# One residual quantiser on one core: 26 rounding copies change engine, and every queue gets a new order

## The chip, the core and the metric

The kernel runs on one core of one Trainium2 chip. The metric is device time in microseconds from the start to the end of one execution; a kernel's time is the median of several executions. All data are bf16 except the sums in PSUM, which are f32.

The engines are called by the names of the profile: PE is TensorE (matrix products), PEld its weight loads, DVE is VectorE, ACT is ScalarE, POOL is GpSimd, SP is SyncE, which here only issues DMAs. Each engine takes its instructions in the order in which the program lists them, so an instruction that has to wait holds back all that stands behind it on that engine.

## The reference

`x` is 2 x 16000 x 512. A depthwise convolution of three taps and a SiLU make `z`; four codebooks of eight words each quantise it in turn, each the residual that the one before left; a second depthwise convolution of three taps decodes the sum of the chosen words.

```
z = silu(conv3(x, dw_enc))
res = z ; q = 0
for s in range(4):
    cb = codebooks[s]                         # 8 x 512
    d2 = sum(res*res) - 2*res@cb.T + sum(cb*cb)
    sel = cb[d2.argmin(-1)]
    q += sel ; res -= sel
y = conv3(q, dw_dec)
```

The squared norm of the residual takes part in the distance, rounded to bf16 as in the reference, and so can decide between words; that is why the kernel computes it.

## The kernel before, in words

The 32,000 rows are laid out as 250 groups of 128. They are worked on in 18 chunks: one of 4 groups, one of 12, thirteen of 16 (numbers 2 to 14), two of 12 (15 and 16) and one of 2 (`SIZES`). Several chunks are under way at once, in different steps:

1. **Load** (L671, SP): transposing DMAs bring a chunk in as XT, with the 512 features on partitions in four blocks.
2. **Front** (L738 to L765), for each of the four blocks: DVE makes the three products of the encoder's taps (L738). One sum of two products is made by an accumulating DMA that POOL issues (L744), the other by DVE (L746). ACT takes the exponential (L750), DVE (or ACT, L755) adds one (L757), ACT takes the reciprocal (L368), DVE multiplies (L765) into RES, the residual. Exponential and reciprocal are in different function tables, and ACT loads a table at each change.
3. **Four stages**, s = 0 to 3, on RES. PE makes products of the residual with the code words and with itself in groups of rows, into PSUM (L839, L844). What follows has two forms. In chunks of 16 groups (`apart`): ACT moves the products of the residual with itself into GRAM (L855) and the dot products into PR (L879), PE adds up both in PSUM, with L865 and L871 as its last step; so one PSUM tile holds, for each row and each of the eight words, the norm plus the dot product. **A rounding copy then takes this 128x128 tile out of PSUM into V as bf16.** In all other chunks DVE takes the norm by a reduction (L875) and adds it to PR in L922. From V on, DVE adds the words' norms (L927), takes the minimum of eight (L932) and marks where it stands (L937). PE turns the marks (L963 or L949), ACT copies them out (L972), PE makes pairs of them (L999), ACT copies these out (L1004), PE multiplies them with the code words (L1032), and DVE takes the chosen words from RES (L1039, or L1043 in small chunks), four instructions a stage. Then the next stage's products can begin. The last stage has no subtraction: its marks go on to the decoder (L976 to L989).
4. **Decode** (L1061, L1067, L1071): PE multiplies the marks with code words times decoder taps, ACT copies the result to YSB, SP stores it.

The rounding copy is the one instruction whose engine the change touches. `copied` (in `stage`) decides it: `COPIES` has one number for chunks with an even number and one for odd ones, and bit s of it says whether ACT makes the copy in stage s.

```
copied = apart and COPIES[st["n"] % 2] >> s & 1
...
if apart:
    if copied:
        nc.scalar.activation(u["V"]..., u["N"], ACT.Copy)       # L917
    else:
        nc.vector.tensor_copy(u["V"]..., u["N"])                # L919
    return
```

`apart` needs a chunk of four times four groups (`MB >= LEAST`, with `LEAST` = 4), a bit of `NORMS` (15, so all stages) and a chunk number from `NFROM` = 0 to below `NTO` = 15. With `COPIES = (5, 5)`, bits 0 and 2, ACT makes the copies of stages 0 and 2 and DVE those of stages 1 and 3: 26 each, for 13 chunks.

The order in which the program lists its steps is written out in full: each step (a product, an exponential, a stage's products of one group of rows, one subtraction, one transposing DMA) is a task with a number, and `ORDER` is a list of all 3,217 numbers. `Plan.run` goes down the list and emits each task's instructions, so the list fixes the order on every engine, SP's and POOL's DMA issues included. It also contains entries of -1, at which PE gets a matrix product without use (L612), meant to keep it busy, if one can be placed. The list must name a task after those that it needs.

```
for n in ORDER:
    if n < 0:
        self.idle()
        continue
    tasks[n][5]()
```

Buffers in turns limit how far chunks can run ahead: 2 tiles of XT, 6 of Z, 4 of T, 4 of E, 3 of RES, 2 of YSB; in PSUM 2 small tiles hold a stage's products and sums (`psG`), 3 large ones everything else (`psA`). The rounding copy is what frees the small tile in which the sums stand.

Of the kernel before, what the change touches and what calls it, by code (L numbers as in the profile page):

```python
# [63 lines left out]
NTO = 15  # L64
LEAST = 4
COPIES = (5, 5)
# [260 lines left out]
def kernel(  # L327
# [489 lines left out]
    def stage(st, s, due):  # L817
# [5 lines left out]
        seen, maxima, grams = [], [], []  # L823
        apart = MB >= LEAST and NORMS[st["n"] % 2] >> s & 1 and NFROM <= st["n"] < NTO

# [339 lines left out]
```

## Time and profile before

| | us |
|---|---|
| three executions | 654.52, 656.47, 660.09 |
| their median | 656.47 |
| the profiled execution, whole | 654.74 |
| its span, first to last instruction | 653.0 |
| in the span DVE was busy | 614.3 |
| ACT | 581.7 |
| PE | 509.0 |

The profiled execution is thus 1.73 us below the median; 1.74 us of it lie outside the span. The mean clock granted to TensorE was 0.934 of full speed.

Busy time of an engine is the time in which at least one of its instructions ran. Instructions of one engine overlap a little at their ends, so the sum of their durations is larger than the busy time; what one more instruction takes of a full queue is read from the distance between two starts. In a row of a group, the number behind the bar is the busy time of the group in us, then the mean duration of one in ns; behind the second bar stands how long the engine was idle just before such instructions, and what ended that idle time.

### The profile page before, as it was taken

Reading aid. Unit: us, or ns where it says so; the run is one execution under the profiler, and the core shown is the slowest. Engines: PE = TensorE matmul, PEld = TensorE weight load, DVE = VectorE, ACT = ScalarE, POOL = GpSimd, SP = SyncE. Lnnn points to the kernel's source line nnn. Section 1 sums busy time; section 2 is a strip of 40 time slices with the busy share of each in tenths; the row PEclk is TensorE's granted clock in tenths of the full one; section 3 lists DMA queues with packets and bytes.
Section 4 is the critical chain, followed back from the end, with each engine's and each line's share of the span. In section 5 each row is a group of like instructions: output and inputs, shape, how many; then the busy total and the mean of one; then the engine's idle time right before and its main releaser. Section 6 shows DMA issues by size and latency. Waiting matters only on the chain.

```text
span 653.0 us, 25437 instructions
## 1 busy us (share of the span) xinstructions
PE 509.0 (78%) x11302; PEld 319.6 (49%) x11389; DVE 614.3 (94%) x991; ACT 581.7 (89%) x862; POOL 93.1 (14%) x133
## 2 busy tenths in 40 slices
PE   4115674777878799888988798888779888999985
PEld 3114452534545455555655455545445555556552
DVE  7999999999989999999999999999999999999872
ACT  3887857799889999999999999999999999997576
POOL 7403111111101201011011101111111111200000
PEclk9656677989989999999999999999999999999999
DMA  9949886899898999998799989999889936242234
GB/s 202 134 93 183 150 137 128 135 156 151 167 152 148 185 207 166 192 190 182 142 230 159 158 206 164 175 182 212 148 178 166 174 92 171 86 140 72 92 140 186
DMA packets 148489, 103.33 MB, mean 158 GB/s; under 512 B 130169, under 2 KB 131194, under 8 KB 148250
## 3 DMA queue, kind: packets, MB, share of 16 engines
q1 hardware_dynamic: 137076, 65.96, 50.8%
q0 software_dynamic: 11296, 35.73, 33.1%
q8 instruction: 89, 1.46, 0.9%
q14 instruction: 22, 0.18, 0.1%
q10 hardware_dynamic: 6, 0.00, 0.0%
HBM read 3.61 MB, written 32.77 MB: 56 GB/s over the span
## 4 chain that ended last, share of the span: by engine, by line
DVE 37%; ACT 32%; PE 13%; DMA 7%; SPq 6%; issue 5%; DVEq 0%; ACTq 0%; POOLq 0%
DVE RES L1039 9%; ACT YSB L1067 8%; ACT E L368 7%; DVE T L738 6%; SPq L671 5%; ACT E L750 5%; PE PS L844 5%; PE SEL L1032 4%; DVE RES L1043 4%; DVE Z L746 4%; DVE RES L765 4%; ACT GRAM L855 3%; DMA Z<-T 3%; DMA out_dram<-YSB 3%; DVE Z L738 3%
## 5 line engine op out<-in xcount | busy, mean ns | idle before, releaser
L844 PE MATMUL PS<-RES 128*64 128x80 bf16 (+1 forms) x8064 | 187.2, 205 | 25.2 <-DVE RES L765 13.7
L844 PEld LDWEIGHTS <-RES 128*64 128x64 bf16 x8064 | 161.5, 116 | 80.9 <-issue 46.0
L1039 DVE TENSOR_TENSOR RES<-RES,SEL 128x2048 bf16<-128x2048 bf16 x156 | 186.4, 1216 | 7.8 <-PE SEL L1032 7.5
L1032 PE MATMUL SEL<-OHP,W 64*128 64x512 bf16 (+2 forms) x1296 | 157.3, 365 | 28.3 <-ACT OHP L1004 10.6
L744 POOL DMA_DIRECT2D Z<-T x72 | 69.3, 975 | 480.3 <-DVE T L738 88.1
L1067 ACT ACTIVATE YSB<-Y 128x1024 bf16<-128x1024 f32 (+1 forms) x126 | 130.2, 1049 | 7.8 <-PE Y L1061 4.8
L750 ACT ACTIVATE E<-Z 128x2048 bf16<-128x2048 bf16 (+2 forms) x72 | 122.9, 1718 | 4.2 <-DVE Z L746 3.4
L368 ACT ACTIVATE E<-E 128x2048 bf16<-128x2048 bf16 (+2 forms) x72 | 122.9, 1723 | 1.5 <-DVE E L757 1.3
L738 DVE TENSOR_SCALAR T<-XT,WENC 128x2048 bf16<-128x2048 bf16 (+2 forms) x144 | 97.3, 686 | 2.1 <-DMA Z<-T 2.1
L1032 PEld LDWEIGHTS <-W 64*128 64x128 bf16 x1296 | 57.2, 97 | 80.1 <-issue 43.9
L765 DVE TENSOR_TENSOR RES<-Z,E 128x2048 bf16<-128x2048 bf16 (+2 forms) x72 | 78.2, 1086 | 0.1
L855 ACT ACTIVATE GRAM<-PS 128x384 bf16<-128x384 f32 (+1 forms) x156 | 73.0, 489 | 5.6 <-PE PS L844 5.4
L746 DVE TENSOR_TENSOR Z<-Z,T 128x2048 bf16<-128x2048 bf16 (+2 forms) x72 | 74.3, 1040 | 1.0 <-DMA Z<-T 1.0
L839 PE MATMUL PS<-MASK,IDENT 128*128 128x384 bf16 (+1 forms) x188 | 61.0, 325 | 12.6 <-POOL MASK L482 5.1
L1061 PE MATMUL Y<-A,FIN 128*128 128x512 bf16 x173 | 57.3, 382 | 13.3 <-ACT FIN L989 2.8
L879 ACT ACTIVATE PR<-PS 128x48 bf16<-128x48 f32 (+1 forms) x188 | 41.1, 235 | 17.0 <-PE PS L844 13.0
L1043 DVE TENSOR_TENSOR RES<-RES,SEL 128x1536 bf16<-128x1536 bf16 (+1 forms) x60 | 42.9, 738 | 7.1 <-PE SEL L1032 7.1
L738 DVE TENSOR_SCALAR Z<-XT,WENC 128x2048 bf16<-128x2048 bf16 (+2 forms) x72 | 48.4, 676 | 0.0
L1004 ACT ACTIVATE OHP<-ps_pair,NEG 128x512 bf16<-128x512 f32 (+2 forms) x54 | 35.6, 659 | 4.2 <-PE ps_pair L999 4.0
L757 DVE TENSOR_SCALAR E<-E 128x2048 bf16<-128x2048 bf16 (+2 forms) x63 | 38.6, 626 | 0.4 <-ACT E L750 0.4
L839 PEld LDWEIGHTS <-IDENT 128*128 128x128 bf16 x188 | 18.2, 97 | 33.5 <-issue 25.5
L937 DVE TENSOR_TENSOR OH<-V,M 128x128 bf16<-128x128 bf16 x72 | 31.5, 437 | 0.6
(103 smaller groups left out, 455.7 us busy)
## 6 DMA issues: line engine op xcount, KB each, us to landing
out_dram<-YSB SPq DMA_DIRECT2D x61, 512.0 KB, 3.9
Z<-T POOLq DMA_DIRECT2D x58, 512.0 KB, 5.8
XT<-in_x_dram SPq DMA_TRANSPOSE x233, 4.5
Z<-T POOLq DMA_DIRECT2D x9, 384.0 KB, 5.2
RES<-in_x_dram SPq DMA_DIRECT2D x1, 1536.0 KB, 10.3
RES<-in_x_dram SPq DMA_DIRECT2D x1, 640.0 KB, 5.8
Z<-T POOLq DMA_DIRECT2D x5, 128.0 KB, 3.1
W<-in_codebooks_dram POOLq DMA_DIRECT2D x6, 64.0 KB, 10.9
```

Of the source, the lines that this page charges most:

```text
L368: nc.scalar.add_instruction(mybir.InstActivation(name=nc.get_next_instruction_name(), engine=mybir.EngineType.Activation, ins=args, outs=[ ...
L738: nc.vector.tensor_scalar(out=places(u[name]), in0=taps(i, k), scalar1=WENC[:, i, k:k + 1], scalar2=None, op0=ALU.mult)
L744: nc.gpsimd.dma_start(out=z, in_=t, accum_op=ALU.add)
L746: nc.vector.tensor_tensor(out=z, in0=z, in1=t, op=ALU.add)
L750: nc.scalar.activation(u["E"][:, 0:G, :], u["Z"][:, 0:G, :], ACT.Exp, scale=-1.0)
L765: nc.vector.tensor_tensor(out=st["RES"][:, i, 0:2 * G, LC:LC + HT], in0=halves(u["Z"]), in1=halves(u["E"]), op=ALU.mult)
L839: nc.tensor.matmul(V[:, :, own:own + HT], lhsT=IDENT, rhs=MASK[:, 0:m, :], start=True, stop=False, skip_group_check=True)
L844: nc.tensor.matmul(V[h * HT:(h + 1) * HT, e, :], lhsT=half[:, LC:LC + HT], rhs=half[:, lo:hi], start=False, stop=(i == KT - 1), skip_group ...
L855: nc.scalar.activation(u["G", q][:, 0:m, :], u["V", q][:, :, own:own + HT], ACT.Relu)
L1032: nc.tensor.matmul(SEL[:, r, 0:R * HT], lhsT=WORDS[s][k][rows, i * P:(i + 1) * P], rhs=u["OHP"][rows, 0:R * HT], start=(k == 0), stop=(k = ...
L1039: nc.vector.tensor_tensor(out=now, in0=now, in1=sel.rearrange("p (h q t) -> p h q t", h=2, t=HT)[:, :, 0:G, :], op=ALU.add)
L1067: nc.scalar.activation(u["YSB"][:, k:k + n, :], u[k][:, 0:n, :], ACT.Copy)
```

## The change

The diff has three parts.

```
-NTO = 15
+NTO = 17
-COPIES = (5, 5)
+COPIES = (0, 0)
 ORDER = [
-    0, 1, 43, 326, 44, 170, 171, 2, 5, 9, 3, 34, 18, 26, 10, 8, -1, -1, 7, 41, 39, 4, 6, 47,
...
+    0, 1, 43, 326, 44, 170, 171, 2, 5, 3, 34, 9, 26, 18, 10, 4, 6, 41, 8, 7, 35, 51, 47, 52,
...
 ]
```

`COPIES = (0, 0)` gives DVE the rounding copies of all four stages: L917 is no longer reached, and L919 (L918 in the changed kernel, whose list is one line shorter) is reached 52 times.

`NTO` rises from 15 to 17. Chunks 15 and 16 have 12 groups, and `apart` asks for 16.

`ORDER` is another list. It names the same 3,217 tasks; it has 11 entries of -1 in place of 30. In the built programs ACT has 26 instructions fewer, DVE 26 more, PE four matrix products of L612 fewer with their weight loads (10 in place of 14). All other instructions are the same in kind, shape and number on each engine, ACT's table loads, POOL's accumulating DMAs and SP's loads and stores among them, and stand in another order.

269 rows, old and new, of the table ORDER are left out of this document.

## The prediction

> **What bounds the kernel now.** I read the page's busy shares first, then a table of busy time by stretches of the span, then the chain of waits, then DVE's waits.
>
> ```profile
> span 653.0 us, 25437 instructions
> ...
> PE 509.0 (78%) x11302; PEld 319.6 (49%) x11389; DVE 614.3 (94%) x991; ACT 581.7 (89%) x862; POOL 93.1 (14%) x133
> ```
>
> ```profile
> core 0: us, PE busy (x) PEld busy (x) DVE busy (x) ACT busy (x) POOL busy (x), PEclk, DMA share, GB/s
> 0.00:20.00 20.00, 8.31 (x81) 7.55 (x82) 15.46 (x52) 9.47 (x10) 15.12 (x42) 1.00 0.97 195
> 20.00:120.00 100.00, 47.28 (x915) 32.97 (x915) 99.82 (x175) 75.59 (x93) 18.32 (x27) 0.64 0.80 137
> 120.00:200.00 80.00, 61.49 (x1344) 37.37 (x1352) 74.21 (x106) 69.25 (x95) 8.70 (x10) 0.91 0.99 152
> 200.00:560.00 360.00, 310.81 (x7252) 192.78 (x7311) 353.86 (x505) 355.65 (x545) 44.94 (x45) 1.00 0.96 173
> 560.00:600.00 40.00, 38.78 (x909) 23.96 (x919) 37.30 (x72) 35.83 (x64) 6.07 (x9) 1.00 0.36 105
> 600.00:653.00 53.00, 42.30 (x808) 25.01 (x817) 33.68 (x86) 35.94 (x62) 0.00 (x0) 0.99 0.33 131
> ```
>
> By the whole span DVE is the fuller engine, 94% against 89%. By stretches it is not so simple. From 20 to 120 us DVE is full (99.82 of 100) and ACT has a quarter of its time free. From 200 to 560 both are full, and ACT slightly more: it is idle for 4.35 us of 360, DVE for 6.14. After 560 PE comes near its limit (38.78 of 40), and after 600 nobody is full: that is the tail of the last chunks, one step after the other.
>
> ```profile
> DVE 37%; ACT 32%; PE 13%; DMA 7%; SPq 6%; issue 5%; DVEq 0%; ACTq 0%; POOLq 0%
> ```
>
> The chain that ended last changes between the two all the time, DVE with 37% of the span and ACT with 32%. So the kernel is bound by two engines that are matched to each other, and work moved from one to the other is paid at one rate and refunded at a similar one.
>
> ```profile
> DVE RES L1039 <- PE SEL L1032: 7.5, 12, 2.7
> DVE RES L1043 <- PE SEL L1032: 7.1, 8, 3.1
> ...
> DVE V L919 <- PE PS L871: 1.3, 2, 1.1
> ```
>
> DVE's named waits (total us, times, longest) are few. The 26 rounding copies that DVE has already waited for their sums twice, 1.3 us together.
>
> **The change part by part.** *NTO* changes nothing: the only chunks it could add have 12 groups, and the built program has no instruction more for it. What it costs is nothing, with nothing to cover.
>
> *26 copies leave ACT and come to DVE.*
>
> ```profile
> L917 ACT ACTIVATE V<-PS 128x128 bf16<-128x128 f32 x26 | 8.6, 329 | 1.3 <-PE PS L871 1.3
> ...
> L919 DVE CAST V<-PS 128x128 bf16<-128x128 f32 x26 | 7.3, 282 | 1.3 <-PE PS L871 1.3
> ```
>
> ```profile
> 20.00:120.00 100.00, 0.27 (x1) 0.64 0.80 137
> 120.00:200.00 80.00, 1.11 (x4) 0.91 0.99 152
> 200.00:560.00 360.00, 6.91 (x20) 1.00 0.96 173
> 560.00:600.00 40.00, 0.28 (x1) 1.00 0.36 105
> ```
>
> The second of these tables is ACT's L917 alone, by the same stretches: 20 of the 26 lie where both engines are full and only one where DVE alone is. A duration is not what a copy takes of a full queue, since neighbours overlap. That is read from starts:
>
> ```profile
> 202.50 0.28 DVE L919 CAST V<-PS 128x128 bf16<-128x128 f32 x1
> 202.70 0.75 DVE L738 TENSOR_SCALAR T<-XT,WENC 128x2048 bf16<-128x2048 bf16 x1
> ...
> 219.38 0.28 DVE L919 CAST V<-PS 128x128 bf16<-128x128 f32 x1
> 219.70 0.22 DVE L927 TENSOR_TENSOR V<-V,GPOS 128x128 bf16<-128x128 bf16 x1
> 219.84 1.22 DVE L746 TENSOR_TENSOR Z<-Z,T 128x2048 bf16<-128x2048 bf16 x1
> ...
> 239.09 0.22 DVE L927 TENSOR_TENSOR V<-V,GPOS 128x128 bf16<-128x128 bf16 x1
> 239.35 0.29 DVE L932 TENSOR_REDUCE M<-V 128x16 bf16<-128x128 bf16 x1
> ```
>
> ```profile
> 315.75 0.33 ACT L917 ACTIVATE V<-PS 128x128 bf16<-128x128 f32 x1
> 315.91 1.08 ACT L1067 ACTIVATE YSB<-Y 128x1024 bf16<-128x1024 f32 x1
> ```
>
> On DVE a copy takes 0.20 us (202.50 to 202.70) if the next instruction doesn't need it, 0.32 (219.38 to 219.70) if it does. On ACT it takes 0.16 (315.75 to 315.91), or its duration of 0.33 at most, where the next can't overlap it. So DVE gets 26 x 0.20 = 5.2 us (ends: 5.2 and 26 x 0.32 = 8.3), and ACT loses 26 x 0.16 = 4.2 (ends: 4.2 and 26 x 0.33 = 8.6). I take the lower end on both sides, since both queues are full there and mostly have something else to run next.
>
> *The new list on DVE.* An instruction that reads what the one just before it wrote starts later by 0.12 us: 0.32 against 0.20 for L919 above, and 0.26 (239.09 to 239.35) against 0.14 (219.70 to 219.84) for L927. In the built programs DVE has 64 such neighbours before and 49 after. That gives back 15 x 0.12 = 1.8 us, and DVE's queue is longer by 5.2 - 1.8 = 3.4 us.
>
> *What of that is on the path.* If DVE set the pace throughout, +3.4; if ACT did, -4.2. By their shares of the chain, 37 to 32, it is 0.54 x 3.4 - 0.46 x 4.2 = -0.1, that is nothing.
>
> *The new waits.* An ACT copy whose sums are late holds back ACT's exponentials; a DVE copy whose sums are late holds back DVE's subtractions and sums of products, and with them PE's next stage and ACT's next exponential. On DVE's side a gain is excluded: no wait of L927 for L917 is among DVE's waits, so there is none to remove. The copies already there waited 1.3 / 26 = 0.05 us each; at that price 26 more cost 1.3, and ACT gets its own 1.3 of L917 back. But the list matters more. I counted DVE's work, at the starts of this trace, between the last instruction that writes a stage's residual and the copy that needs its sums. Before, the shortest of DVE's 26 had 7.3 us, after, three have 5.9, 6.1 and 6.8. If 7.3 was just enough, these wait (7.3 - 5.9) + (7.3 - 6.1) + (7.3 - 6.8) = 3.1 us; if it was ample, nothing. I take half, +1.5.
>
> *The rest of the list* I cost at nothing. Four useless products fewer:
>
> ```profile
> L1067 ACT ACTIVATE YSB<-Y 128x1024 bf16<-128x1024 f32 (+1 forms) x126 | 130.2, 1049 | 7.8 <-PE Y L1061 4.8 <-DMA out_dram<-YSB 0.9 <-PE SEL L1032 0.7
> ...
> L612 PE MATMUL PS<-CB,IDENT 128*128 128x512 bf16 x12 | 4.1, 383 | 0.2 <-issue 0.2
> ```
>
> 4 x 0.383 = 1.5 us of PE, hidden in the first 120 us behind a full DVE; without that cover PE's clock (0.64 there) could be slower for want of work, and PE has 52 us free before it matters. SP's first store stands behind 77 transposing loads instead of 67, its fifth behind 100 in both; the two YSB buffers cover it, and without them ACT's wait for a store, 0.9 us in all now, would grow. POOL's accumulating DMAs are as many. The tail has the same instructions on DVE in nearly the same order. How well the list as a whole fits is the real unknown: DVE is idle for 0.18 + 5.79 + 6.14 us from 20 to 560, so a perfect list gains no more than those 12 us, and one that leaves DVE idle for half as much again loses 6.
>
> The sum: 654.74 - 0.1 + 1.5 = 656.1 for an execution like the profiled one. That one lay 1.73 us below the median of its runs, so I put the median at 656.1 + 1.7 = 657.8, say **658.0**. Its own range, by the ends of the prices (+3.4 + 3.1 above, -4.2 below) around 656.5, is about 652 to 663.
>
> For the two prices by copy: the Trainium skill, "VectorE: DVE Perf Modes", section "The TRN2 errata", gives (120 + 128) / 0.96 GHz = 258 ns for DVE and (172 + 128) / 1.2 GHz = 250 ns for ACT to take 128 elements out of PSUM, as an estimate from its table. The trace has 282 and 329, so here it is DVE that is the cheaper; by the Trainium skill's figures the move would cost 26 x 8 ns = 0.2 us more than it frees, and the sum would be 656.3 in place of 656.1.
>
> **The rivals.**
>
> *DVE pays in full (slower).* DVE sets the pace in every stretch, so all that is added to it lengthens the run: 26 x 0.282 = 7.3, no neighbour saved; 656.47 + 7.3 = 663.8. For it: 99.82 of 100 early, 94% overall. Against it: 20 of 26 copies lie where ACT is the fuller. The Trainium skill, "Perfetto Trace Analysis", sections "Identifying the Most-Contended Engine" and "Optimizing Scalar/DVE Operations", says the same as a rule: work on the engine with the highest occupancy first, and if DVE is saturated, move work to ACT. This change does the opposite. The trace agrees with it from 20 to 120 us and not from 200 to 560.
>
> *The copies stand at the head of DVE's queue and wait (slower).* At a mean wait of 0.3 us for 26 copies, between the 0.05 of now and the longest of 1.1: 3.4 + 7.8 = 11.2, so 667.7. It decides from (6.6 - 3.4) / 26 = 0.12 us each, where the loss passes 1%. For it: the three short covers. Against it: 26 copies in the same place do it already at 0.05.
>
> *ACT sets the pace (faster).* Then its 26 durations come out, 8.6 us: 656.47 - 8.6 = 647.9, or 652.3 if only 4.2 come out. For it: 355.65 of 360. Against it: 75.59 of 100 early, and 37% of the chain on DVE.
>
> *Nothing that counts is changed.* NTO does nothing, the copies cancel, the list is as good as the old: 656.5.
>
> **How the numbers follow.** The three runs of before lie within 0.9% of each other, so 1%, 6.6 us, is about what a measurement can tell from no change. Forecast 0.45 (of which 0.05 slower and 0.01 faster by over 1%); DVE pays in full 0.12 (half of it over 1%); copies wait 0.18 (0.17 over); ACT sets the pace 0.17 (0.11 faster by over 1%); nothing changes 0.08. Faster 0.12, slower 0.28, within 1% 0.60. The range runs from 650, which leaves out half of the ACT case, 0.09, to 668, which leaves out half of the waiting case, 0.09.
>
> **What would show it.** In the profile of the changed kernel: DVE's busy time about 619, ACT's about 573; L918 52 times at about 0.28 with an idle time before it of 2 to 4 us. From 200 to 560 us' worth of work DVE should now be the fuller of the two, and its share of the chain should rise above 37%. An idle time before L918 of 8 us or more would show the waiting rival; a DVE share that stays and a span shorter by 4 or more, the ACT rival. I am wrong if the span moves by over 6 us with L918's waits small: then it is the rest of the list, and the place would be seen in the table by stretches.

## The result, and the profile after

| | median, us | lowest to highest | executions | ratio of the times, 95% interval |
|---|---|---|---|---|
| before | 657.18 | 654.52 to 661.56 | 8 | |
| after | 666.24 | 661.47 to 666.57 | 8 | 1.0118 [1.0093, 1.0143] |

The changed kernel is slower by 1.2%. Medians here and below are of all executions, while the ratios leave disturbed ones out, so a ratio can differ a little from the quotient of two medians.

The profiled execution of the changed kernel took 661.47 us, 659.8 of it span. It is the fastest of the eight, 4.8 us below their median, so its trace shows only a part of the loss: its span is 6.8 us longer than that of before. This is the head of its page:

```profile
span 659.8 us, 25480 instructions
...
PE 508.3 (77%) x11303; PEld 322.8 (49%) x11385; DVE 617.7 (94%) x1017; ACT 579.1 (88%) x836; POOL 91.5 (14%) x133
...
ACT 20%; DVE 19%; DMA 8%; PE 8%; issue 5%; SPq 4%; POOL 0%; DVEq 0%; ACTq 0%; POOLq 0%
```

DVE's busy time rose from 614.3 to 617.7, by 3.4 us. The span rose by 6.8, so DVE also sat idle for 659.8 - 617.7 = 42.1 us in place of 38.7, that is 3.4 more. Half of this trace's loss is work on DVE, half is idle time on DVE. ACT's busy time fell by 2.6. The last line, the chain that ended last, adds up to 64% of the span, since it was not followed back to the start; its shares can't be set against the 37% and 32% of before.

The stretches of the span, with the columns of before (us, busy time and count of PE, PEld, DVE, ACT, POOL, then the clock granted to PE, DMA share, GB/s):

```profile
0.00:20.00 20.00, 8.61 (x82) 7.92 (x82) 14.32 (x51) 9.48 (x9) 15.68 (x46) 1.00 0.97 200
20.00:120.00 100.00, 46.08 (x911) 32.59 (x914) 98.13 (x173) 74.87 (x93) 17.89 (x24) 0.66 0.80 135
120.00:200.00 80.00, 59.93 (x1361) 38.06 (x1363) 78.01 (x114) 70.81 (x96) 8.89 (x10) 0.94 0.91 158
200.00:560.00 360.00, 308.56 (x7162) 192.80 (x7213) 349.30 (x516) 348.12 (x514) 43.09 (x45) 0.99 0.96 171
560.00:600.00 40.00, 36.98 (x831) 22.44 (x840) 38.24 (x72) 34.16 (x57) 5.98 (x9) 1.00 0.35 104
600.00:660.00 60.00, 48.12 (x963) 28.98 (x974) 39.74 (x95) 41.68 (x73) 0.00 (x0) 0.99 0.31 125
```

From 200 to 560 us DVE is idle for 10.7 us (6.1 before) and ACT for 11.9 (4.3 before). Both engines lost time there together, which a mere move of work from one to the other would not do. DVE's waits (total us, times, longest):

```profile
DVE T L737 <- DMA Z<-T: 4.6, 4, 1.4
...
DVE T L737 <- issue: 3.0, 2, 2.7
...
DVE V L918 <- PE PS L870: 0.4, 2, 0.2
```

The copies hardly wait: 0.4 us for all 52, less than the 1.3 of before. The waits for accumulating DMAs (Z<-T) are 6.8 us in all, with 2.2 ahead of L745, where the kernel before has 3.1. What is new is one wait of 2.7 us ahead of a product of the encoder's taps (L737); "issue" means that this view found nothing that ended it. It lies here, on DVE's timeline:

```profile
351.51 0.28 DVE L918 CAST V<-PS 128x128 bf16<-128x128 f32 x1
354.51 0.75 DVE L737 TENSOR_SCALAR T<-XT,WENC 128x2048 bf16<-128x2048 bf16 x1 [2.71 <-issue]
```

And on the chain of waits around it (start, us, what), which follows SP's transposing loads:

```profile
347.76 4.03 DMA XT<-in_x_dram
351.80 2.52 issue
354.31 0.05 DVEq L737
```

This product is the first that reads a newly loaded chunk. The chain of the kernel before passes the same place of the same chunk:

```profile
346.87 4.55 DMA XT<-in_x_dram
351.42 0.04 DVEq L738
```

There DVE's queue moves on within 0.04 us of the load's landing. After the change it passes the same place 2.9 us later. The 2.52 us that the view calls "issue" have a reason, which the semaphore events of the same trace show: from 351.48 to 354.26 us DVE's queue stands at the semaphore of that very load, and the last of the load's 16 signals comes at 354.23. The 351.80 of the view is only the end of the copy that was still running. Both kernels wait at this place for the 160th load. Before, it was issued at 346.87 and landed at 351.42, after 4.6 us; now it was issued at 347.76 and landed at 354.23, after 6.5 us. So it was issued 0.9 us later and took 1.9 us longer. An accumulating DMA issued at 347.54 was under way beside it until 353.83; that this is what held it up is not shown.

What followed is seen in slices of 10 us of the changed kernel, with their sum from 320 to 400 us:

```profile
350.00:360.00 10.00, 6.65 (x137) 3.73 (x134) 7.02 (x12) 7.44 (x9) 0.86 (x1) 0.92 1.15 177
360.00:370.00 10.00, 8.88 (x211) 5.53 (x210) 9.09 (x14) 8.64 (x13) 1.75 (x2) 0.91 0.94 188
370.00:380.00 10.00, 6.49 (x172) 4.42 (x173) 10.00 (x15) 9.97 (x12) 0.86 (x1) 0.95 1.19 172
380.00:390.00 10.00, 9.53 (x194) 5.85 (x196) 9.70 (x17) 10.00 (x20) 0.86 (x1) 0.88 1.01 161
...
sum 80.00, PE 66.31 PEld 41.46 DVE 75.05 ACT 74.03 POOL 7.77; mean PE 8.29 PEld 5.18 DVE 9.38 ACT 9.25 POOL 0.97
```

and the first of these slices before, with the sum of the same 80 us:

```profile
350.00:360.00 10.00, 7.87 (x180) 5.32 (x182) 9.60 (x15) 9.59 (x15) 1.28 (x1) 1.00 0.92 178
...
sum 80.00, PE 68.93 PEld 43.31 DVE 78.47 ACT 78.89 POOL 10.15; mean PE 8.62 PEld 5.41 DVE 9.81 ACT 9.86 POOL 1.27
```

DVE did 3.4 us less work in these 80 us, ACT 4.9 less. For DVE that is as much as the whole of this trace's extra idle time; elsewhere gains and losses cancel. The DMA share, the column before the last, is between 0.94 and 1.19 in the four slices from 350, and between 0.80 and 1.19 in the same slices before. The DMAs were nearly as loaded before the change, so the share alone doesn't say why this load came late.

### The profile page after: what moved, and what is told of

Same layout as the page of the kernel before. It is cut to its first block, busy times and chain, and to the rows that moved or that the text cites. A ratio compares the mean times of both kernels' runs of the same rounds, so it can differ in the third digit from the quotient of the medians.

```text
span 659.8 us, 25480 instructions
## 1 busy us (share of the span) xinstructions
PE 508.3 (77%) x11303; PEld 322.8 (49%) x11385; DVE 617.7 (94%) x1017; ACT 579.1 (88%) x836; POOL 91.5 (14%) x133
## 4 chain that ended last, share of the span: by engine, by line
ACT 20%; DVE 19%; DMA 8%; PE 8%; issue 5%; SPq 4%; POOL 0%; DVEq 0%; ACTq 0%; POOLq 0%
DVE RES L1038 6%; ACT YSB L1066 5%; ACT E L749 4%; DMA Z<-T 4%; SPq L670 4%; ACT E L367 3%; DMA out_dram<-YSB 3%; PE SEL L1031 3%; PE PS L843 3%; ACT GRAM L854 2%; DVE T L737 2%; DVE RES L764 2%; DVE Z L745 2%; DMA XT<-in_x_dram 1%; DVE RES L1042 1%
## 5 line engine op out<-in xcount | busy, mean ns | idle before, releaser
L743 POOL DMA_DIRECT2D Z<-T x72 | 67.9, 970 | 490.8 <-DVE T L737 84.8
L737 DVE TENSOR_SCALAR T<-XT,WENC 128x2048 bf16<-128x2048 bf16 (+2 forms) x144 | 96.2, 678 | 7.8 <-DMA Z<-T 4.6
L745 DVE TENSOR_TENSOR Z<-Z,T 128x2048 bf16<-128x2048 bf16 (+2 forms) x72 | 74.4, 1041 | 2.3 <-DMA Z<-T 2.2
L737 DVE TENSOR_SCALAR Z<-XT,WENC 128x2048 bf16<-128x2048 bf16 (+2 forms) x72 | 48.6, 678 | 0.0
L756 DVE TENSOR_SCALAR E<-E 128x2048 bf16<-128x2048 bf16 (+2 forms) x63 | 38.7, 619 | 0.2 <-ACT E L749 0.2
L962 PE MATMUL ps_oh<-IDENT,OH 128*64 128x64 bf16 x204 | 16.1, 233 | 29.4 <-DVE OH L936 27.6
```

The lines of the kernel that those rows point to most:

```text
L737: nc.vector.tensor_scalar(out=places(u[name]), in0=taps(i, k), scalar1=WENC[:, i, k:k + 1], scalar2=None, op0=ALU.mult)
L743: nc.gpsimd.dma_start(out=z, in_=t, accum_op=ALU.add)
L745: nc.vector.tensor_tensor(out=z, in0=z, in1=t, op=ALU.add)
```

## The experiments

Each kernel was compared with the kernel before on the same chip. Lines are one lower in kernels with the new list than in those with the old one (L918 is L919).

**after_again** is the changed kernel once more, with no edit.

> The changed kernel once more, for a second profile: the first profiled execution (661.47) was the fastest of eight, the median is 666.24. Theory of late loads (SP's transposing loads stand behind stores, and DVE waits for a chunk's rows): this profile shows one or more waits of DVE's first product of a chunk (L737) of 2 us or over, as the 2.7 us near 352 us in the first profile, and each execution that is slower has more of them. Theory of the longer queue (DVE simply has 3.4 us more to do and ACT gets nothing back): no single wait of DVE over 2 us from 60 to 600 us, the same DVE busy time (618), and the span longer by small waits everywhere.

Ratio 1.0102 [1.0058, 1.0146], median of ten 667.28 us. The profiled execution took 658.38 and again was the fastest of its group. The head of its page:

```profile
span 656.6 us, 25562 instructions
...
PE 517.1 (79%) x11385; PEld 321.1 (49%) x11385; DVE 618.1 (94%) x1017; ACT 579.7 (88%) x836; POOL 90.7 (14%) x133
```

And among DVE's waits in it:

```profile
DVE V L918 <- PE PS L870: 1.8, 3, 0.9
```

The span is 3.6 us longer than that of before, DVE's busy time 3.8, its idle time 656.6 - 618.1 = 38.5 against 38.7. Between 60 and 600 us no wait of DVE is over 2 us, as the theory of the longer queue has it. In this pair of traces, without a long stall, the loss is just what DVE was given; as executions of the kernel before lie up to 7 us apart, one pair doesn't prove that nothing comes back from ACT. Loads are late here too: by the semaphore events DVE waits 1.9 us for them, up to 0.9 at once. Both traced executions are the shortest of their groups; a typical one takes 5 to 7 us more (4.8 in the first group, 6.5 among the executions that the ratio here counts) and was never caught in a profile.

**copies_alone** is the kernel before with the first two parts of the change and the old list.

```
-NTO = 15
+NTO = 17
-COPIES = (5, 5)
+COPIES = (0, 0)
```

> All 52 rounding copies on DVE, but the old list. Queue theory: DVE has 26 x 0.20 = 5.2 us more and no neighbours saved, so about 657.2 + 5 = 662 (ratio 1.008). Theory of late loads: the loads stand as in the kernel before, so at most the 37-to-32 balance, about 657 to 659 (ratio 1.000 to 1.003). If the moved copies wait for their sums at places meant for ACT: 668 or more.

Ratio 1.0171 [1.0122, 1.0219], median 668.26 us. The head of its page, and the wait of its copies:

```profile
span 666.9 us, 25550 instructions
...
PE 525.5 (79%) x11389; PEld 322.1 (48%) x11389; DVE 620.9 (93%) x1017; ACT 580.2 (87%) x836; POOL 93.9 (14%) x133
```

```profile
DVE V L919 <- PE PS L871: 4.7, 5, 1.8
```

Here the copies stand on DVE where ACT's copies stood in the list. In the built program 19 of the 52 are followed at once by the addition that needs them, against 7 of 26 before: 12 neighbours more. By the prices read from starts that is 26 x 0.20 + 12 x 0.12 = 6.6 us more on DVE, and its busy time rose by 6.6. The waits of the copies for their sums rise from 1.3 to 4.7, and DVE's idle time in the span by 46.0 - 38.7 = 7.3. This is the last of the three outcomes that were expected, the copies at places meant for ACT.

**list_alone** has the new list and the copies as before.

```
-COPIES = (0, 0)
+COPIES = (5, 5)
```

> The new list with the copies of stages 0 and 2 back on ACT. Queue theory: DVE has 1.8 us less than before and ACT the old work: 655 to 657 (ratio 0.997 to 1.000). Theory of late loads: the list carries the loss, so 663 to 667 (ratio 1.009 to 1.015).

Ratio 1.0466 [1.0415, 1.0518], median 687.91 us. One of ACT's waits in its trace, and one of DVE's:

```profile
ACT V L916 <- PE PS L870: 15.5, 16, 2.4
```

```profile
DVE V L926 <- ACT V L916: 6.1, 3, 3.0
```

Both theories foretold 667 us at most, and both missed by over 20. In the new list the copies come at places that suit DVE. Given back to ACT, they stand at the head of ACT's queue for 15.5 us, and DVE waits for them too. A list is good or bad only together with its `COPIES`: with the copies on DVE the new list is the better one (1.010 to 1.012 against 1.017, by little more than the intervals), with the copies shared the old one (1 against 1.047).

**list_sp_before** is the changed kernel with SP's tasks, loads and stores, in the sequence of the old list; the other engines keep the new one.

```
 ORDER = [
-    0, 1, 43, 326, 44, 170, 171, 2, 5, 3, 34, 9, 26, 18, 10, 4, 6, 41, 8, 7, 35, 51, 47, 52,
...
```

> The changed kernel with the order of the old list on SP alone (loads and stores); DVE, ACT, PE and POOL keep the new order. Theory of late loads: 3 to 8 us come back, 658 to 663, and the 2.7 us wait of DVE near 352 us is gone. Queue theory: 666, as the changed kernel, within 2. If the new list's stores fit the old SP order badly, ACT's wait for a store (L1066 for the output's DMA, 2.7 us now) grows by as much as it loses.

Ratio 1.0378 [1.0328, 1.0428], median 681.66 us. A wait of DVE in its trace, and one of ACT:

```profile
DVE Z L737 <- DMA XT<-in_x_dram: 6.8, 2, 6.3
```

```profile
ACT YSB L1066 <- DMA out_dram<-YSB: 9.6, 5, 3.7
```

DVE waits 6.3 us for one load, and ACT's copies into YSB wait 9.6 us for stores (0.9 before, 2.7 after the change). The theory of late loads foretold a gain of 3 to 8 us, and the opposite came. SP's sequence was said to cost nothing because two YSB buffers cover it. It is anything but free: exchanged alone, it costs about 2.6% on top of the changed kernel (1.0378 against 1.0118), twice what the whole change does. What this shows is that SP's sequence and the rest of the list have to fit each other, not that the old sequence is the worse one.

**act_copies_dropped** is the kernel before without ACT's 26 copies; the addition behind them reads the sums in PSUM itself.

```
     if copied:
-        nc.scalar.activation(u["V"]..., u["N"], ACT.Copy)
+        return
...
-    ... in0=u["V"]...
+    ... in0=u["N"] if copied else u["V"]...
```

> The kernel before with the old list; the 26 copies of stages 0 and 2 are left out, so ACT has 26 instructions less and DVE none more: DVE adds the words' norms (L927) straight from PSUM, which leaves out the rounding of those sums to bf16 and costs DVE some 26 x 0.06 = 1.6 us for the slower source. By the prediction's step (what ACT gives back counts for its share of the chain, 46% of 4.2 us): 1 to 3 us faster, ratio 0.995 to 0.999. If ACT's refund is worth nothing, because DVE sets the pace: 657 to 660, ratio 1.000 to 1.004. If ACT sets the pace: 4 us faster or more, 0.994 or less.

Ratio 1.0017 [0.9981, 1.0054]. The busy times on its page, and two of its groups of instructions:

```profile
PE 518.3 (79%) x11389; PEld 318.6 (49%) x11389; DVE 615.9 (94%) x991; ACT 579.0 (88%) x836; POOL 95.8 (15%) x133
```

```profile
L927 DVE TENSOR_TENSOR V<-V,GPOS 128x128 bf16<-128x128 bf16 x46 | 10.4, 225 | 0.5
...
L927 DVE TENSOR_TENSOR V<-PS,GPOS 128x128 bf16<-128x128 f32 x26 | 7.5, 290 | 0.0
```

ACT is 2.7 us less busy, as in the changed kernel, and no time is gained. The experiment isn't quite clean: an addition that reads PSUM takes 290 ns in place of 225, and DVE is 1.6 us busier. The run is 1.1 us longer (1.2 shorter to 3.6 longer). If DVE's 1.6 us were paid in full, ACT's 2.7 would have brought back 0.5; if in part, nothing. The prediction's step stood for a ratio of 0.995 to 0.999, a refund of nothing for 1.000 to 1.004, and 1.0017 is among the latter. But by the end of the interval all of it could have come back, so this run alone makes a small refund likely and no more.

**dve_copies_added** is the kernel before with 26 reductions more on DVE, of an unchanging tile, where ACT's copies are used.

```
+    if copied:
+        nc.vector.tensor_reduce(out=EXTRA, in_=CB4[:, 0:GC * C]..., axis=AX.X, op=ALU.min)
```

> The kernel before with the old list and all its copies on ACT as they were; in front of 26 of DVE's L927 stands one more DVE instruction of the same price on its queue (a reduction of 128 columns to 16 of a constant, 0.20 us start to start by L932's rows, without a wait). If DVE pays in full: +5 to +7 us, ratio 1.008 to 1.011, and then the 1.017 of all copies on DVE with the old list has 4 us more for copies that wait for their sums at places meant for ACT. By the prediction's step (54% of 5.2): +3, ratio 1.004. If the whole cost of moving the copies is DVE's time, with stalls that follow from it: +10, 1.015 to 1.018.

Ratio 1.0047 [1.0011, 1.0084], that is 3.1 us (0.7 to 5.5). The busy times on its page:

```profile
PE 525.8 (80%) x11389; PEld 323.8 (49%) x11389; DVE 619.4 (94%) x1017; ACT 582.8 (88%) x862; POOL 94.7 (14%) x133
```

DVE's busy time rose by 5.1 us, so about six tenths of what is added to DVE lengthen the run, with an interval that reaches from little to all of it. That is what the prediction's step has for DVE (54%, foretold as 1.004). By that the 3.4 us on DVE account for some 2 us of the changed kernel's loss, by the interval for 0.5 to all 3.4; the loss is 7.8 us (6.1 to 9.4) by its ratio. The Trainium skill, "Perfetto Trace Analysis", section "Optimizing Scalar/DVE Operations", says that where DVE is saturated, moving some of its work to ACT may make sense. These two runs agree with it, with 1.0047 for the work added to DVE and 1.0017 for the work taken from ACT.

**before_stores_eighth and after_stores_eighth** write only 16 of 128 partitions in each store, in either kernel.

```
-    nc.sync.dma_start(out=outv[:, g:g + len(groups), :], in_=u["YSB"][:, 0:len(groups), :])
+    nc.sync.dma_start(out=outv[0:16, g:g + len(groups), :], in_=u["YSB"][0:16, 0:len(groups), :])
```

> The kernel before, with each store writing 16 of 128 partitions (7/8 of the output are left out), so that the DMA queues carry a third less and loads and accumulating DMAs land earlier. If DMAs bind little in the old list: 652 to 658. If they bind: 645 to 651.

> The changed kernel with the same cut of its stores. Theory of thin DMA margins (in the new list DVE's products wait for loads and for T tiles that accumulating DMAs hold, 3.0 and 6.8 us in the first profile against 0 and 3.1 before): the gap to the old list with the same cut shrinks from 8 or 9 us to 4 or less, what is left being DVE's 3.4 us of more work, and the times of single executions lie closer together. If DMA margins have nothing to do with it: the gap stays at 7 to 10 us.

Before 653.27 us, 0.9922 [0.9887, 0.9958]; after 653.77 us, also 0.9922 [0.9885, 0.9959]. Both ratios are to the unchanged kernel before. With an eighth of the stores' bytes the two kernels are level, to within some 3 us by the intervals, though DVE is still 2.6 us busier after the change (617.4 against 614.8).

**loads_two_earlier and loads_two_later** are the changed kernel with entries of SP moved in the list: in the one, each store lets up to two later loads pass (60 moves); in the other it goes ahead of up to two loads (61 moves).

```
 ORDER = [
...
-    ... 464, 468, 462, 314, 924, 169, ...
+    ... 464, 468, 462, 1276, 1271, 314, 924, 169, ...
```

> The changed kernel; on SP alone each store lets up to two of the transposing loads behind it go first (60 loads moved). Cutting the stores took the whole gap away, so DMAs cause it; which of them is open. If it is the loads, which come late behind stores (first product of a chunk less than 3 us after its last load, in the first profile, for chunks 6, 10, 12 and 14): 2 to 6 us faster than the changed kernel, 660 to 664. If the loads have margin enough and it is the stores that hold ACT up (YSB tiles): 2 to 8 us slower than it. If it is the accumulating DMAs, or the traffic as such: no change, 665 to 668.

> The changed kernel; on SP alone each store goes before up to two of the loads ahead of it (61 loads moved). If loads are what is late: 3 to 10 us slower than the changed kernel, 670 or more, with waits of DVE's first products for XT. If stores are what is late: faster by 2 to 5 us. If neither: no change.

Earlier loads: 1.0188 [1.0140, 1.0235], median 669.23 us. ACT waits for stores:

```profile
ACT YSB L1066 <- DMA out_dram<-YSB: 12.3, 8, 3.3
```

Later loads: 1.0203 [1.0147, 1.0259], median 674.59 us. DVE waits for loads:

```profile
DVE T L737 <- DMA XT<-in_x_dram: 6.5, 2, 4.6
```

The second came out as expected for late loads; the first, which should then have gained, lost. So the new list isn't wrong in one simple direction. Loads that come earlier make the stores late, and the other way round: 2.7 us of waiting for stores becomes 12.3 in the one, and 1.7 in the other, where a load costs 4.6 at once. Neither shift found slack.

**before_sums_eighth and after_sums_eighth** let the accumulating DMAs add only 16 of 128 partitions.

```
-    nc.gpsimd.dma_start(out=z, in_=t, accum_op=ALU.add)
+    nc.gpsimd.dma_start(out=z[0:16], in_=t[0:16], accum_op=ALU.add)
```

> The kernel before with the same cut of the accumulating DMAs, for the comparison: 650 to 657, as with the cut of the stores, if the queues' traffic is what slows it; 657 to 659 if nothing waits for these DMAs.

> The changed kernel with its stores whole, but each accumulating DMA adds 16 of 128 partitions (7/8 of one of the two sums of products are left out for the first product pair of each block), so that these DMAs land sooner and load the queues less. If the gap between the lists comes from waits for accumulating DMAs (T and Z tiles), or from the traffic as such: the gap to the old list with the same cut is 4 us or less. If it comes from SP's own order of loads and stores: the gap stays at 6 us or more.

Before 647.7 us, 0.9840 [0.9806, 0.9874]; after 650.11 us, 0.9883 [0.9843, 0.9922]. The head of the page of each, before and then after:

```profile
span 645.4 us, 25471 instructions
...
PE 504.6 (78%) x11302; PEld 317.8 (49%) x11389; DVE 613.9 (95%) x991; ACT 580.6 (90%) x862; POOL 88.3 (14%) x133
```

```profile
span 646.9 us, 25520 instructions
...
PE 506.9 (78%) x11303; PEld 321.0 (50%) x11385; DVE 616.1 (95%) x1017; ACT 578.0 (89%) x836; POOL 84.6 (13%) x133
```

And the long stretch of each:

```profile
200.00:560.00 360.00, 313.23 (x7313) 194.16 (x7373) 356.29 (x510) 357.97 (x550) 43.32 (x49) 1.00 0.62 118
```

```profile
200.00:560.00 360.00, 315.39 (x7325) 196.74 (x7375) 357.13 (x528) 355.81 (x528) 40.24 (x48) 0.99 0.61 118
```

With the DMA share in this stretch down from 0.96 to 0.62 both kernels lose idle time: DVE's in this stretch goes from 6.1 to 3.7 us before, and from 10.7 to 2.9 after. The gap between the medians falls from 9.1 to 2.4 us, within some 3 us by the intervals; 2.2 us of busy time on DVE (613.9 to 616.1) is as large as that.

## Why the prediction held in part, and where it failed

The time lies inside the range of 650 to 668 but above the forecast's own 652 to 663. That it is inside is luck: the upper end was put at 668 for the waiting copies, which did not come. The steps in turn:

*NTO changes nothing.* The counts of instructions agree with it: 1017 on DVE and 836 on ACT are 26 more and 26 fewer, and no other. It was not run by itself.

*26 copies at 0.20 us, 15 dependent neighbours fewer at 0.12: +3.4 on DVE.* Right to the digit in the first trace (+3.4), +3.8 in the second. Reading the price from the distance of two starts held twice, for copies_alone gives 6.6 by the same rule and measured 6.6. ACT's 26 x 0.16 = 4.2 was too much: its busy time fell by 2.6 and by 2.0, less even than the lower end. The signs to look for named 619 for DVE and 573 for ACT, which are not the sum's own +3.4 and -4.2 (617.7 and 577.5); measured were 617.7 and 579.1.

*"That is nothing."* This step failed in one of its halves. It let ACT's saving cancel DVE's cost by the two engines' shares of the chain, and took the 355.65 busy us of 360 as a sign that ACT sets the pace there. DVE's half came out: work added to it was paid by six tenths (1.0047 [1.0011, 1.0084], foretold 1.004). ACT's half did not: the work taken from it gained nothing that could be measured (1.0017 [0.9981, 1.0054], foretold 0.995 to 0.999, which only the edge of the interval reaches). So, as far as these runs tell, an engine can be busy nearly all the time and yet not set the pace; a share of the chain says through whom the last path went, not what it would gain if that engine had less to do. The term should have been about +2 (0.5 to 3.4) in place of -0.1. Pairs of the two kernels don't fix it better: 3.6 us of span for 3.8 of DVE in the second trace, 2.4 us for 2.2 with the sums cut, but 0.5 us for 2.6 with the stores cut, each with some 3 us of uncertainty or more.

*The new waits, +1.5.* 0.4 us in one trace and 1.8 in the other, where 1.3 had been: about nothing. The short covers of 5.9, 6.1 and 6.8 us did no harm that the waits would show.

*"The rest of the list I cost at nothing."* This failed too, and is the larger part. The prediction named how well the list fits as the real unknown and gave it up to 6 us of loss, but priced it from DVE's idle time alone and took SP's order as covered. The chain that it quoted had 13% on the DMAs and their queue (7% DMA, 6% SPq), and the long stretch a DMA share of 0.96: a third resource, of which the sum has no term. What is shown: with less DMA traffic of either kind the gap of 9 us shrinks to 0.5 and 2.4; SP's sequence alone can move the time by several per cent; and the one long stall of the first trace is a wait for a load. The traces add where the new list differs. By the semaphore events, DVE never waits for a load in five of the six traces with the old list, and for 0.4 us in the sixth (act_copies_dropped). In all eight with the new list or a variant of it DVE does wait, from 0.3 us with the sums cut to 9.8 with the loads moved later, and for 3.0 and 1.9 us in the changed kernel itself. Of the 7.8 us of the ratio, DVE's work has some 2 (0.5 to 3.4), and the rest, some 6 (4.4 to 7.3), hangs on how the new list stands against the DMAs. That the loss hangs on the DMAs is shown by the runs; that this rest is one cause and not several small ones is not.

*The useless products.* Their 1.5 us of PE were put into the first 120 us. In the trace of before they run from 192.9 to 645.7 us, seven of the twelve that it shows after 639. The four fewer were not run by themselves.

*From the profiled execution to the median, +1.7.* This did not carry over: the two profiled executions lay 4.8 and 6.5 us below the medians of the executions that the ratios count.

*The rivals.* DVE pays in full was right that nothing comes back from ACT, as far as the runs tell; its price of 7.3 us was twice what DVE got, and of such work some six tenths were paid. The waiting copies came nearest in time, 667.7, for a reason that the traces refute: L918's waits were to be 8 us or more. ACT sets the pace falls by the sign of the result, though ACT did lose its 26 copies; nothing changes falls by its interval. The prediction's own sign for the rest of the list, a span that moves by over 6 us with L918's waits small, came true in the first trace (6.8 with 0.4), and the place was seen in the stretches as it said. There DVE is now the fuller of the two, 349.30 against 348.12, as foretold, but both are less busy than before.

*What stays open.* Which DMA makes the typical execution of the changed kernel late, since only its fastest executions were profiled, and why the late load took 6.5 us. Whether PE's lower clock adds to the loss or only follows from it: of the eight executions two took 664.15 us, one at a mean clock of 0.915 and one at 0.933, so the clock alone doesn't order them. Six of the eight have a mean clock of 0.915 to 0.925, the profiled one 0.932. A third XT buffer, which would give the loads more room, was not tried. No version tried is faster than the kernel before with all of the work done.

## What to carry to other kernels

Where two engines are both full, as here, charge what is added to the one and credit nothing for what is taken from the other, until a run with that work left out shows a gain. Give the DMA queues a term of their own when an order changes: their share in the full stretch and the margins between a landing and its first reader, not only the engines' idle time. An order of instructions belongs to one assignment of work: the new assignment alone was 1.7% slow, the new order alone 4.7%, both together 1.2%.

## What was not expected of the hardware

Accumulating DMAs slowed engines that hardly waited for them by name. DVE's waits for them in the kernel before:

```profile
DVE T L738 <- DMA Z<-T: 2.1, 3, 1.3
...
DVE Z L746 <- DMA Z<-T: 1.0, 2, 0.5
```

These are 3.1 us, yet with an eighth of their bytes the kernel took 1.6% less, some 10 us. The trace with the sums cut shows where much of it came back. DVE's wait for the products with the code words falls from 7.5 us to this:

```profile
DVE RES L1039 <- PE SEL L1032: 2.3, 6, 0.8
```

From 120 to 200 us, where 5.8 of 80 us were idle, DVE has no idle time left:

```profile
120.00:200.00 80.00, 63.90 (x1464) 39.57 (x1473) 80.00 (x116) 74.96 (x105) 8.51 (x11) 0.96 0.62 98
```

Over the whole span DVE's idle time falls by 7.2 us, from 38.7 to 31.5. So most of what these DMAs cost doesn't stand in waits that are named after them.

After the stall of 2.7 us on DVE, PE's granted clock was 0.92, 0.91, 0.95 and 0.88 in slices of 10 us, with 1.00 in the same slices before. Narrower stretches of the same trace show what these means are made of:

```profile
355.04:358.45 3.41, 0.66 (x8) 0.41 (x10) 3.41 (x8) 0.85 (x5) 0.53 (x1) 1.00 1.45 141
358.45:361.87 3.42, 3.42 (x43) 1.76 (x41) 3.42 (x4) 2.45 (x2) 0.33 (x1) 0.50 0.91 185
375.53:378.94 3.41, 1.58 (x57) 1.16 (x55) 3.41 (x6) 3.38 (x6) 0.86 (x1) 1.00 0.97 178
378.94:382.35 3.41, 3.19 (x64) 2.49 (x59) 3.38 (x6) 3.41 (x7) 0.86 (x1) 0.50 0.92 117
```

The clock is at half for two stretches of 3.41 us and full otherwise. Ahead of the first PE was busy for 0.66 of 3.41 us, ahead of the second for 1.58. The Trainium skill, "TensorE: Matmul & The Clock Gate", part 1, has the gate halve the clock after an idle window of about 3.4 us. The trace agrees with the half and with the 3.4 us, but PE was not wholly idle ahead of either stretch. A stall of DVE is not needed for it: in the second trace of the changed kernel such a stretch begins at 370.38 us, with DVE busy for the whole of the 3.41 us ahead of it and PE for 1.98.
